# 400 slots for each expert in place of 432, in a fused kernel of attention and two feed-forward layers

## The chip, the core and the metric

The program runs on one core of a Trainium2 chip. The metric is the device time of one execution in microseconds (us). Engines are named as in the profile: PE is TensorE's matmuls and PEld its weight loads, DVE is VectorE, ACT is ScalarE, POOL is GpSimd, SP is SyncE, and a q behind a name is that engine's queue of instructions that wait, branch or issue a DMA.

## The reference

Three layers follow one another. Only what is computed matters here:

```python
# 1: attention within hash buckets; q, k, v are (2, 8, 768, 64)
mask = q_bucket[:, :, :, None] == k_bucket[:, :, None, :]
scores = np.where(mask, scale * np.matmul(q, k.transpose(0, 1, 3, 2)), -1e9)
attn = softmax(scores); x = np.matmul(attn, v)          # then (1536, 512)
# 2: a feed-forward layer, 512 -> 2048 -> 512
h = x @ w_in; g = h * sigmoid(1.702 * h); x = g @ w_out
# 3: 8 experts, each token goes to two of them
noisy_logits = x @ w_gate + np.log1p(np.exp(x @ w_noise)) * noise
top2 = np.argpartition(-noisy_logits, 2, axis=1)[:, :2]  # weights: softmax of the two
for e in range(8):
    h = np.maximum(x[mask] @ w1[e], 0.0)                 # 512 -> 1024
    out[mask] += top2_w[mask, k, None] * (h @ w2[e])     # 1024 -> 512
```

There are 1536 tokens and two experts for each, so 3072 rows of expert work, 384 for an expert on average. With the reference's own draw of the inputs (seed 0) the eight experts get 375, 391, 391, 396, 364, 373, 395 and 387 of them.

## The kernel before

**Precision.** Operands are split into two fp16 parts, hi and lo, and a product is three matmuls (hi by hi, hi by lo, lo by hi), accumulated in PSUM.

**Attention and the first feed-forward layer** run interleaved over six chunks of 256 tokens (2 batches by 3). A loop over g hands out the work in steps: scores (L252, tile s), row maximum (L261), exponential (L271), hi and lo of it (L310, L319, tile er), a transposing DMA from SP's queue (L323, et from er), and the product with v (L364, tile pv). Of the feed-forward layer L456 makes h, L474 and L486 the activation, L467 makes px. Beside this, SP loads and VectorE converts w_in and w_out, and SP writes zeros into the DRAM buffer slots (L550, L552, four blocks of 128 rows in a step) and into the output (L556). Up to step 100 (GM; the attention has 96 steps) the order on each engine is set by a scheduler that works through a timeline of its own; behind that the order is the order of the code.

**Routing** (from L572) makes the logits of a chunk, takes the two best experts and works out a slot: expert e owns rows e*CAP to e*CAP+CAP-1 of slots; tokens past CAP go to rows behind E*CAP. POOL scatters the token rows (1032 numbers of 2 bytes) into slots with an indirect DMA (L679).

**The experts.** For each expert SP loads the token rows transposed (L749, xg from slots) and their token numbers and weights (L754, L759, tile mt). The first layer L792 makes ph, 128 features by all slots of the expert, 12 matmuls for one of 8 slices; ScalarE and VectorE take it out as ht hi and lo (L802, L803). The second layer makes py for 128 slots at a time (L814, 24 matmuls of 512 columns); the slots past the last whole 128 are done as two halves of 256 columns with 64 slots each (L818, 48 matmuls). ScalarE scales py (L828) and POOL adds the rows to the output with an indirect DMA (L830). Expert 0 is done in two parts, slots 0 to 255 ahead of the last chunk's routing and the rest behind it; experts 1 to 7 are done in one. The weights w1 and w2 of the next expert are loaded (L721, L724) and split (L735, L736) under the current one. All of this stands in an order written by hand.

```python
def parts(e):
    return ((0, REG), (REG, CAP)) if e < EA else ((0, CAP),)      # REG = 256, EA = 1
...
nc.tensor.matmul(ph[:, :c1 - c0], w[:, ws, d * FE + f * 128:d * FE + f * 128 + 128],
                 xg[e, p][:, xs * HP + d, :], ...)                # L792; c0, c1 = parts(e)[p]
...
for i in range(-(-E * CAP // 512)):
    at(PARAM["I0"] + PARAM["IS"] * i, init_slots, i)              # 512 rows of slots in a step
...
most = nc.values_load(cnt_i[0:1, E:E + 1], min_val=0, max_val=N)
with tc.If(most > CAP):                                           # the overflow rows
```

**The overflow.** At the end a branch runs only if some expert has more than CAP tokens. It loads such an expert's weights again through one buffer, gathers up to 128 overflow rows at a time, and does both layers for them (from L1034 on).

Of the kernel before, what the change touches and what calls it, by code (L numbers as in the profile page):

```python
# [20 lines left out]
FF = 2048  # L21
E = 8
FE = 1024
CAP = 432
REG = 256
OV = N - CAP
NF = CAP // 128
NR = CAP - 128 * NF
NO = N + 128 + 64 - NR
# [30 lines left out]
def fused(ctx: ExitStack, tc: tile.TileContext, q, k, v, proj, w_in, w_out, w_gate, w_noise, noise,  # L60
# [451 lines left out]
    iota_e = consts.tile([128, 3, E], F32)  # L512
    for i, (b0, st_) in enumerate(((0, 1), (0, CAP), (7 * CAP, OV - CAP))):
        nc.gpsimd.iota(iota_e[:, i], pattern=[[st_, E]], base=b0, channel_multiplier=0,
# [31 lines left out]
    def init_slots(i):  # L546
        sl = slots[i * 512:min(i * 512 + 512, E * CAP)].rearrange("(k p) c -> p k c", p=128)
        n = sl.shape[1]
        for k_ in range(n):
            nc.sync.dma_start(sl[:, k_, :2 * DM].rearrange("p (u c) -> p u c", c=256),  # L550
                              zeros[:, None, :].to_broadcast([128, 2 * DM // 256, 256]))
        nc.sync.dma_start(sl[:, :, 2 * DM:], blank[:, None, :].to_broadcast([128, n, ROW - 2 * DM]))  # L552
# [13 lines left out]
    def route(ci):  # L566
# [56 lines left out]
        for c in range(2):  # L623
# [36 lines left out]
        yield  # L660
        nc.vector.scalar_tensor_tensor(ov, pq, float(CAP), iota_e[:, 2:3].to_broadcast([128, CT, E]),
                                       op0=OP.is_ge, op1=OP.mult)
# [478 lines left out]
```

## Time and profile before

| what | us |
|---|---|
| median of 3 runs | 852.13 (850.34 to 854.86) |
| the profiled execution | 851.51 |
| its span, first to last instruction | 849.4 |
| TensorE busy | 734.0 (86%) |
| VectorE busy | 541.0 (64%) |
| ScalarE busy | 443.5 (52%) |
| GpSimd busy | 270.9 (32%) |
| mean granted TensorE clock | 0.956 of 2.4 GHz |

The profile is of one execution. Its page gives busy shares over the whole span, which mixes three stages; so the span is also cut into stretches, and for the last stage the chain of waits tells which work followed which without a break. Times in the trace count from the first instruction.

The granted clock has two levels, 1.0 (2.4 GHz) and 0.5 (1.2 GHz); a stretch's figure is the mean. A matmul's own record overlaps those of its neighbours, so the time that a row of matmuls takes is read from the chain, and a record's duration is not its spacing.

### The profile page before, as it was taken

How to read it: one execution, taken by the hardware profiler on the slowest of the kernel's cores; microseconds unless marked ns; L12 is line 12 of the kernel's file. 1: busy time of each engine (PE TensorE's matmuls, PEld its weight loads, DVE VectorE, ACT ScalarE, POOL GpSimd, SP SyncE). 2: the span in 40 equal slices, each digit the busy share in tenths (PEclk: the TensorE clock that was granted, in tenths of full speed). 3: DMA queues.
4: the chain of work that ended last, by engine and by line, in shares of the span. 5: the costliest groups of instructions: out<-in, count | busy, mean ns of one | idle time of the engine just before them, and what ended most of it. 6: DMA issues, size and time to landing. Idle time of an engine off the chain costs nothing. (4 is left out here: it accounts for less than half of the span.)

```text
span 849.4 us, 14814 instructions
## 1 busy us (share of the span) xinstructions
PE 734.0 (86%) x5398; PEld 447.3 (53%) x5399; DVE 541.0 (64%) x1327; ACT 443.5 (52%) x859; POOL 270.9 (32%) x272
## 2 busy tenths in 40 slices
PE   1577658878988989798999999879999999999994
PEld 1354336435754665475567585556455554545542
DVE  8998679987896888568778527444543625335110
ACT  3777657657766686467467335244443434425210
POOL 6355437743334154214312143041021121211212
PEclk9988979998999999989999999989999999999997
DMA  8999998998999999976777634587865757766212
GB/s 205 227 253 230 210 223 179 220 212 173 179 155 214 161 190 194 223 134 106 149 131 122 139 108 122 177 200 167 221 145 168 209 120 194 156 172 162 38 15 36
DMA packets 285453, 141.03 MB, mean 166 GB/s; under 512 B 231552, under 2 KB 264384, under 8 KB 285376
## 3 DMA queue, kind: packets, MB, share of 16 engines
q1 hardware_dynamic: 278848, 126.37, 68.4%
q0 software_dynamic: 6528, 13.68, 9.2%
q8 instruction: 43, 0.70, 0.4%
q14 instruction: 34, 0.28, 0.1%
HBM read 61.49 MB, written 24.25 MB: 101 GB/s over the span
## 5 line engine op out<-in xcount | busy, mean ns | idle before, releaser
L792 PE MATMUL ph<-xg,ew 128*128 128x432 f16 (+2 forms) x864 | 146.8, 334 | 8.7 <-DMA xg<-slots 8.7
L456 PE MATMUL h<-xt,wi 128*128 128x256 f16 x1152 | 139.8, 276 | 2.0 <-DVE th L486 1.7
L467 PE MATMUL px<-wo,gt 128*128 128x512 f16 x576 | 134.9, 388 | 7.2 <-ACT wo L441 3.9
L736 DVE SCALAR_TENSOR_TENSOR ew<-w,ew 128x1024 f16<-128x1024 f32 x64 | 78.0, 1228 | 89.9 <-ACT ew L735 89.9
L830 POOL DMA_INDIRECT out_dram<-yo,ti x32 | 51.9, 1621 | 232.4 <-ACT yo L828 163.1
L814 PE MATMUL py<-ew,ht 128*128 128x512 f16 x576 | 125.8, 379 | 0.0
L456 PEld LDWEIGHTS <-wi 128*128 128x128 f16 x1152 | 112.1, 99 | 24.8 <-issue 5.5
L792 PEld LDWEIGHTS <-ew 128*128 128x128 f16 x864 | 85.3, 101 | 68.3 <-issue 6.4
L252 PE MATMUL s<-kt,qt 128*128 128x512 f16 (+1 forms) x384 | 90.6, 362 | 18.6 <-ACT e L271 14.6
L271 ACT ACTIVATE e<-s,mx 128x768 f32<-128x768 f32 x96 | 85.7, 894 | 34.0 <-DVE mx L262 19.7
L501 POOL TENSOR_TENSOR gt<-th,gt 128x512 f16<-128x512 f32 x48 | 60.2, 1254 | 114.9 <-ACT gt L500 111.3
L467 PEld LDWEIGHTS <-gt 128*128 128x128 f16 x576 | 55.9, 99 | 73.7 <-issue 10.6
L261 DVE TENSOR_REDUCE mx<-s 128x1 f32<-128x768 f32 x96 | 90.7, 949 | 6.3 <-PE s L252 6.1
L814 PEld LDWEIGHTS <-ht 128*128 128x128 f16 x576 | 56.3, 98 | 67.2
L319 DVE SCALAR_TENSOR_TENSOR er<-e,mx,er 128x768 f16<-128x768 f32 x68 | 71.2, 1049 | 24.3 <-ACT er L310 22.6
L310 ACT ACTIVATE er<-e,mx 128x768 f16<-128x768 f32 x68 | 63.3, 934 | 38.1 <-DMA et<-er 24.2
L802 ACT ACTIVATE ht<-ph 128x432 f16<-128x432 f32 (+2 forms) x72 | 35.3, 490 | 82.2 <-PE ph L792 82.2
L803 DVE SCALAR_TENSOR_TENSOR ht<-ph,ht 128x432 f16<-128x432 f32 (+2 forms) x72 | 40.0, 556 | 55.3 <-ACT ht L802 54.6
L828 ACT ACTIVATE yo<-py,wv 128x512 f32<-128x512 f32 (+1 forms) x32 | 20.3, 633 | 103.3 <-PE py L814 54.7
L735 ACT ACTIVATE ew<-w 128x1024 f16<-128x1024 f32 x64 | 66.3, 1047 | 2.5 <-DMA w<-in_moe_w_dram 2.5
L364 PE MATMUL pv<-et,vt 128*64 128x256 f16 x720 | 53.8, 283 | 13.9 <-DMA et<-er 13.9
L252 PEld LDWEIGHTS <-qt 128*128 128x128 f16 x384 | 37.1, 104 | 49.0 <-issue 26.5
(192 smaller groups left out, 930.0 us busy)
## 6 DMA issues: line engine op xcount, KB each, us to landing
w<-in_moe_w_dram SPq DMA_DIRECT2D x64, 512.0 KB
wraw<-in_moe_w_in_dram SPq DMA_DIRECT2D x16, 512.0 KB
wraw<-in_moe_w_out_dram SPq DMA_DIRECT2D x16, 512.0 KB
slots<-zeros SPq DMA_DIRECT2D x27, 256.0 KB
v<-in_v_dram SPq DMA_DIRECT2D x24, 192.0 KB
out_dram<-zeros SPq DMA_DIRECT2D x13, 256.0 KB
k<-in_k_dram SPq DMA_DIRECT2D x16, 192.0 KB
q<-in_q_dram SPq DMA_DIRECT2D x48, 64.0 KB
```

Source lines behind the costliest of these rows:

```text
L252: nc.tensor.matmul(ps[:, n0 * 128:n1 * 128], qt[:, s, h, t, :], kt[:, s, h, n0:n1, :].rearrange("p c t -> p (c t)"), start=(s == 0), stop= ...
L261: nc.vector.reduce_max(mx[:, 0:1], st[g]["ps"][:, :S], axis=AX.X)
L271: nc.scalar.activation(e32, st[g]["ps"][:, :S], AF.Exp, scale=0.125, bias=st[g]["mx"][:, 1:2], accum_out=sms[b, cc, hp][:, 2 * h + t:2 * h ...
L310: nc.scalar.activation(er[:, 0], st[g]["e"], AF.Copy, scale=r)
L319: nc.vector.scalar_tensor_tensor(er[:, 1], d["e"], d["mx"][:, 3:4], er[:, 0], op0=OP.mult, op1=OP.subtract)
L456: nc.tensor.matmul(ph[:, a, :], wi[ws][:, d, f0:f0 + 128], xt[:, d, xs, :], start=(d == 0 and ws == 0 and xs == 0), stop=(d == HP - 1 and ...
L467: nc.tensor.matmul(px, gts[ci, f // 2][:, gs, f % 2, t * 128:t * 128 + 128], wo[ws][:, f, :], start=(f == 0 and gs == 0 and ws == 0), stop ...
L501: nc.gpsimd.tensor_tensor(gt[:, 1], th, gt[:, 0], op=OP.subtract)
L735: nc.scalar.activation(hi, x, AF.Copy, scale=SW1 if j == 0 else SW2)
L736: nc.vector.scalar_tensor_tensor(lo, x, SW1 if j == 0 else SW2, hi, op0=OP.mult, op1=OP.subtract)
L792: nc.tensor.matmul(ph[:, :c1 - c0], w[:, ws, d * FE + f * 128:d * FE + f * 128 + 128], xg[e, p][:, xs * HP + d, :], start=(d == 0 and ws = ...
L814: nc.tensor.matmul(py, ht[:, f, hs, t * 128:t * 128 + 128], w[:, ws, f * DM:(f + 1) * DM], start=(i == 0), stop=(i == n - 1))
```

## The change

CAP goes from 432 to 400. What is worked out from it changes with it: OV, the rows for one expert's overflow, from 1104 to 1136; NF, the whole tiles of 128 slots, stays 3; NR, the slots past them, goes from 48 to 16; NO, the rows of the output with its padding, from 1680 to 1712. No instruction of the experts is added or taken away; they have other shapes.

```diff
 E = 8
 FE = 1024
-CAP = 432
+CAP = 400
 REG = 256
 OV = N - CAP
 NF = CAP // 128
```

In the order of the instructions three places matter.

SP's queue, in the attention part, at the last step of init_slots (before; slots are the expert rows in DRAM, qt, er and et belong to attention, xrt to the routing):

```order
L550 DMA slots<-zeros 128x4x256 x3
L552 DMA slots<-blank 128x3x8
L167 DMA_TRANSPOSE qt<-qsa 128x4x128
L323 DMA_TRANSPOSE et<-er 128x12x128 x2
L167 DMA_TRANSPOSE qt<-qsa 128x4x128
L120 DMA q_2247<-in_q_dram 128x128 x2
L323 DMA_TRANSPOSE et<-er 128x12x128 x2
L124 DMA k_2442<-in_k_dram 128x384
```

The same place now:

```order
L550 DMA slots<-zeros 128x4x256
L552 DMA slots<-blank 128x8
L167 DMA_TRANSPOSE qt<-qsa 128x4x128
L323 DMA_TRANSPOSE et<-er 128x12x128 x2
L167 DMA_TRANSPOSE qt<-qsa 128x4x128
L120 DMA q_2245<-in_q_dram 128x128
L323 DMA_TRANSPOSE et<-er 128x12x128
L120 DMA q_2245<-in_q_dram 128x128
```

Two of the zeroing writes are gone (3200 rows are 6 steps of four blocks and one block), and from here on the loads of q and k and the transposes of et stand in another order.

TensorE, shortly behind that place (before; pb is for the hash buckets, wo and gt make px):

```order
L178 LDWEIGHTS qt
L178 MATMUL pb<-pq,qt 128x6
L364 LDWEIGHTS vt
L364 MATMUL pv<-et,vt 64x256
L252 LDWEIGHTS qt
L252 MATMUL s<-kt,qt 128x512
L252 LDWEIGHTS qt
L252 MATMUL s<-kt,qt 128x256
```

The same place now:

```order
L178 LDWEIGHTS qt
L178 MATMUL pb<-pq,qt 128x6
L467 LDWEIGHTS gt
L467 MATMUL px<-wo_99,gt 128x512
L467 LDWEIGHTS gt
L467 MATMUL px<-wo_98,gt 128x512
L364 LDWEIGHTS vt
L364 MATMUL pv<-et,vt 64x256
```

Matmuls of px have moved ahead of the product with v and of the scores. Blocks of rows are exchanged in this way on every engine until the end of the attention part, and none on TensorE between there and the end of the experts.

SP's queue in the expert part, expert 0's second part and expert 1 (before; w are the raw weights):

```order
L724 DMA w_7146<-in_moe_w_dram 128x2x512
L749 DMA_TRANSPOSE xg<-slots 128x8x176
L754 DMA mt<-slots 128x8
L759 DMA mt<-slots 48x8 x2
L724 DMA w_7224<-in_moe_w_dram 128x2x512
L749 DMA_TRANSPOSE xg<-slots 128x8x432
```

The same place now:

```order
L724 DMA w_7144<-in_moe_w_dram 128x2x512
L749 DMA_TRANSPOSE xg<-slots 128x8x144
L754 DMA mt<-slots 128x8
L759 DMA mt<-slots 16x8 x2
L724 DMA w_7222<-in_moe_w_dram 128x2x512
L749 DMA_TRANSPOSE xg<-slots 128x8x400
```

Here nothing has moved (the weight loads differ by the numbers of their buffers alone); the loads from slots have 32 rows less each.

## Rows read from the trace of the kernel before

**Rows 1.** The page: the span, and busy us, share of it, instructions.

```profile
span 849.4 us, 14814 instructions
...
PE 734.0 (86%) x5398; PEld 447.3 (53%) x5399; DVE 541.0 (64%) x1327; ACT 443.5 (52%) x859; POOL 270.9 (32%) x272
```

**Rows 2.** Busy us by stretch; behind them granted TensorE clock, DMA share, GB/s.

```profile
187.00:250.00 63.00, 54.16 (x476) 37.32 (x475) 54.76 (x167) 46.07 (x97) 24.09 (x23) 0.92 0.95 169
250.00:300.00 50.00, 45.53 (x414) 28.76 (x413) 37.42 (x106) 31.97 (x67) 13.96 (x14) 0.97 1.01 188
300.00:350.00 50.00, 44.54 (x361) 27.52 (x360) 39.57 (x124) 31.71 (x69) 22.70 (x22) 1.00 0.99 201
350.00:400.00 50.00, 42.61 (x369) 30.75 (x368) 36.09 (x90) 31.71 (x67) 15.03 (x15) 0.92 0.78 143
400.00:467.00 67.00, 65.85 (x535) 42.99 (x533) 53.79 (x148) 41.35 (x80) 15.26 (x14) 0.98 0.71 129
...
538.50:567.00 28.50, 23.45 (x162) 15.38 (x163) 14.31 (x57) 9.96 (x21) 8.54 (x9) 0.93 0.62 181
567.00:587.50 20.50, 20.42 (x182) 16.19 (x182) 7.39 (x28) 6.52 (x13) 2.51 (x2) 0.85 0.83 181
...
731.10:767.00 35.90, 35.90 (x219) 18.90 (x218) 15.52 (x26) 14.33 (x20) 6.13 (x5) 1.00 0.72 168
```

**Rows 3.** Chain of waits from 555 us: start, us, what (xN: pieces in a row).

```profile
562.00 5.04 DMA xg<-slots
...
567.08 12.47 PE ph L792 x108
...
695.22 17.63 PE ph L792 x96
712.84 15.54 PE py L814 x72
728.38 2.74 PE py L818 x48
...
818.37 10.37 PE py L814 x48
...
830.18 4.86 DMA out_dram<-yo,ti
```

**Rows 4.** Chain of waits, 500 to 560 us.

```profile
503.41 10.50 PE h L456 x96
...
534.34 4.13 DMA xg<-slots
...
557.84 4.14 DMA slots<-xr,si
```

**Rows 5.** The page's DMA issues: out<-in, queue, count, KB each.

```profile
slots<-zeros SPq DMA_DIRECT2D x27, 256.0 KB
```

**Rows 6.** Timeline of 180 to 193 us: start, us, engine, line, instruction.

```profile
182.07 1.99 SPq L550 DMA_DIRECT2D slots<-zeros  x3
```

**Rows 7.** Busy us by stretch, just ahead of the moved rows (columns as in rows 2).

```profile
150.00:185.00 35.00, 28.82 (x196) 15.43 (x194) 32.66 (x57) 23.16 (x44) 20.46 (x17) 0.95 1.04 226
```

**Rows 8.** TensorE's waits, 187 to 467 us: us in total, times, longest.

```profile
PE pv L364 <- DMA et<-er: 9.0, 7, 4.3
PE s L252 <- ACT e L271: 4.4, 9, 1.0
```

**Rows 9.** Groups by shape: count | busy us, mean ns | idle before, releaser.

```profile
L792 PE MATMUL ph<-xg,ew 128*128 128x432 f16 x672 | 124.0, 346 | 0.0
...
L736 DVE SCALAR_TENSOR_TENSOR ew<-w,ew 128x1024 f16<-128x1024 f32 x64 | 78.0, 1228 | 89.9 <-ACT ew L735 89.9
...
L735 ACT ACTIVATE ew<-w 128x1024 f16<-128x1024 f32 x64 | 66.3, 1047 | 2.5 <-DMA w<-in_moe_w_dram 2.5
...
L792 PE MATMUL ph<-xg,ew 128*128 128x256 f16 x96 | 12.6, 297 | 3.8 <-DMA xg<-slots 3.8
...
L792 PE MATMUL ph<-xg,ew 128*128 128x176 f16 x96 | 10.3, 287 | 4.9 <-DMA xg<-slots 4.9
```

## The prediction

> **What bounds the kernel now.** I read the busy shares first, then the busy time by stretch, then the chain of waits in the stretch that the change touches most, then the groups by shape, and last what TensorE waits for in the attention part.
>
> The page's busy line puts TensorE at 734 of 849.4 us, but that is an average over stages with different limits, so it decides nothing [rows 1]. The stretches do [rows 2]. From 587.5 us to 828.8 us TensorE is busy without a gap, 35.90 of 35.90 us for each expert, at the full granted clock (1.00, 2.4 GHz), while VectorE has 15.5 and ScalarE 14.3 us of work in the same 35.9 and the DMA share is 0.72. Nothing but TensorE's own columns sets the end there. The chain of waits says the same and names the lines [rows 3]: an expert is 96 L792 matmuls in 17.63 us, 72 L814 matmuls in 15.54 us and 48 L818 halves in 2.74 us, one behind the other, with no wait of another engine between them. In front of it, 538.5 to 567 us is a chain of latencies (routing, a scatter into slots, the transposing load xg), and the stretch from 187 to 467 us is a mixed one: TensorE idles 8.8, 4.5, 5.5, 7.4 and 1.2 us in the five rows [rows 2].
>
> **The profiled execution and the median.** That execution took 851.51 us, of which 849.4 are span and 2.1 lie around it; the median shown is 852.13, 0.6 more. I make the sum against 851.51 and add 0.6 at the end.
>
> **The change part by part.** One constant falls from 432 to 400. What follows from it:
>
> *1. L792 on the seven experts that run in one part.* 672 matmuls have 400 columns in place of 432. What a column costs is read from the chain, where the work is end to end: 96 matmuls of 256 columns take 10.50 us, 109.4 ns each [rows 4]; 96 of 432 take 17.63 us, 183.6 ns; 72 of 512 take 15.54 us, 215.8 ns [rows 3]. The slope is 0.422 ns a column from 256 to 432 and 0.402 from 432 to 512. 400 lies in the first interval, so 32 columns are 13.5 ns and 672 of them 9.1 us; by the other slope 8.7 us. I take **9.0 us**. All of it is on the path, since no other engine is near: VectorE and ScalarE work less than half of the period there [rows 2].
>
> The Trainium skill, page "TensorE: Matmul & The Clock Gate", section "Back-to-back issue gap", gives two rules for this: a sustained stream of weight loads and matmuls at about 81 ns a matmul at 128 columns and 131 ns at 512, and for the isolated gap columns over 2.4 GHz plus 2.5 ns. By the first an estimate for 32 columns is 4.2 ns and the 768 changed matmuls would save only 3.2 us; by the second 13.3 ns and 10.2 us. The first speaks against this change; the trace's 215.8 ns at 512 columns agrees with the second and not with the first.
>
> *2. L792 on expert 0's second part.* 96 matmuls go from 176 to 144 columns. The chain shows 108 matmuls in 12.47 us from 567.08 us on, the last 12 of them already expert 1's [rows 3]; without these (12 x 0.1836 = 2.2) the 96 take 10.27 us, 107 ns each, in a stretch whose granted clock is 0.85, so partly at 1.2 GHz. At the full level 32 columns are 13.5 ns, 1.3 us for 96; at the lower one twice that, 2.6. TensorE waited 4.9 us for xg just before, so the low stretch is at the beginning, and time saved there only brings more of the matmuls into it; what falls away at the end runs at the full level. I take **1.3 us**.
>
> *3. Transposing loads and slot zeroing.* Expert 0's second xg is on the chain, 5.04 us for 176 rows, where the first took 4.13 us for 256 [rows 3, 4]. The rows alone would give 5.04 x 32/176 = 0.9 us less; that more rows took less time says that rows are not what it waits for, so the bounds are 0 and 0.9 and I take **0.3 us**. The other seven are issued an expert ahead, under 35.9 us of TensorE's work; if that cover were gone they would cost as much as this one, 5 us each. Of the zeroing, two of 27 writes of 256 KB fall away near 182 us [rows 5, 6]: 0.5 MB at that stretch's 226 GB/s is 2.3 us of the DMA engines' time, at a share of 1.04 [rows 7]. It is a gain only if TensorE's next wait is for a DMA behind them: bounds 0 and 2.3 us, taken as 0, because TensorE waits for transposes of et only 9.0 us in 7 places of the 280 us that follow [rows 8].
>
> *4. Work that shrinks under cover.* L802 and L803, which take L792's result out of PSUM, handle 400 columns; both hide under TensorE's 12 matmuls for the next slice (12 x 0.170 = 2.0 us), and were that cover gone, TensorE would have waits in the chain, where there are none [rows 3]. L814 and L818 keep their counts and shapes: the last tile still covers 64 slots, of which 16 instead of 48 are new. The last scatters, 20.6 us behind the last whole L814 tile, keep their number and size, so the tail behind 828.7 us is moved and not changed.
>
> *5. The order of the attention part.* The missing zeroing makes the scheduler put everything from about 182 us to 480 us into another order, on all engines; the order after that is written by hand and stays. No instruction is added. The rows of the order shown with the change have one unit's pv and scores behind matmuls of px instead of ahead of them; further on the scores stand 20 to 78 rows earlier and h later. That can go either way, and no row of before shows the new order. I bound it by the idle shares of the four rows from 187 to 400 us, 14.0, 8.9, 10.9 and 14.8% [rows 2]. TensorE idles 26.2 of these 213 us; at the best of the shares it would be 19.0 (a gain of 7.2), at the worst 31.5 (a loss of 5.3). I take **0**, since the four rows already are four orders of nearly the same work, and their mean is what stands there now.
>
> **The sum.** 9.0 + 1.3 + 0.3 = 10.6 us. 851.51 - 10.6 = 840.9; with the 0.6 to the median 841.5 us.
>
> **The rivals.**
>
> *The new order costs TensorE more than the old one.* For it: between 187 and 467 us TensorE waits in short pieces for transposes of et and for ScalarE and VectorE [rows 8], and VectorE has 54.8 of 63 us of work in the first row [rows 2], so a row moved forward delays another. Against it: from 400 us on TensorE has a stock of px and h and idles 1.2 us in 67. If 187 to 400 us idled at the 17.7% of the stretch just ahead (28.8 busy of 35 [rows 7]), that is 37.6 us, 11.4 more: **853 us**. Half of that gives 847. Its mirror image, an order that closes the gaps by more than 7.2 us, gives **under 834**.
>
> *Another unit takes over in the expert stage.* The period falls from 35.9 to 34.6 us. Were the 4 MB of weights for each expert already at their limit, the stage would keep its period and only parts 2 and 3 remain: **850.5 us**. Against it: the DMA share is 0.72 in the period shown and VectorE is at 43% [rows 2].
>
> *Columns are cheaper than the chain says.* The mean durations by shape differ by less: 346 ns at 432 columns, 297 at 256, 287 at 176 [rows 9]. By these slopes 32 columns are 8.9 ns, and 4.0 ns between 176 and 256: 6.0 + 0.4 + 0.3 = 6.7 us, **845 us**. The Trainium skill's first rule above (same page and section) points this way. Against it: these records overlap (96 of 346 ns would be 33 us, and the chain fits them into 17.63), so they measure depth and not spacing.
>
> *Slower than before: the overflow path runs.* At the end one branch asks whether any expert has more than 400 tokens. It runs 128 rows of such an expert again, loading all its weights through one buffer. Per expert: 8 times 512 KB at 168 GB/s (3.1 us), L735 (1.05) and L736 (1.23) in turn [rows 2, 9], 43 us; a gather and a transpose at 4.1 and 5.0, 96 matmuls at 107 ns, 24 at 216 ns and a scatter at 4.9 [rows 3, 4], 29 us. Some 70 us on top of 841.5: **912 us**. It decides with the 401st token of one expert. Worked out from the reference's own draw, the experts get 375, 391, 391, 396, 364, 373, 395 and 387 tokens, so four are missing; what speaks for it is only that the kernel's arithmetic may place a token differently, or that another draw is timed. The same number would tell that the change doesn't do what it says.
>
> **How the numbers follow.** Forecast 0.63 (834 to 846.5 us); the new order costs more than 5 us 0.17; it gains more than 7 us 0.08; another unit takes over 0.05; cheaper columns 0.03; overflow 0.04. The likeliest is 841.5. The range from 834 to 850 leaves out most of the gain beyond 7 us (0.07), the dearer half of the order's loss (0.08) and the overflow (0.04). Half a per cent, which is about what a measurement of this kernel can tell from no change, is 4.3 us: faster means under 847.9, slower over 856.4. Faster: 0.63 + 0.08 + 0.03 and a third of the order's loss, 0.78 rounded down; slower: the overflow and the far end of the order's loss, 0.06; the rest, 0.16, is within.
>
> **What the profile after would show.** Part 1: L792 in the chain at 16.3 us for 96, and 34.6 us from one expert to the next at clock 1.00; if it is 17 us or more, the slope is wrong. Part 2: the 108 matmuls in about 11 us. Part 3: xg ahead of them within 4 to 5.1 us. Part 4: L814 and L818 unchanged at 15.54 and 2.74, and some 20.6 us behind the last whole tile. Part 5: the time at which the first L792 matmul starts, 538.5 now; every microsecond by which it starts elsewhere is the order's doing, and the forecast is wrong by just that. Matmuls of the branch at the end would mean the overflow.

## The result

The changed kernel takes 842.83 us (median of 8 runs, 840.05 to 848.53) against 853.07 us of the kernel before (8 runs beside it, 850.34 to 854.86): ratio 0.9888, 95% interval 0.9857 to 0.9918. The forecast was 841.5 us, faster. The profiled execution took 843.4 us, of which 841.3 are span. A ratio is an estimate of its own from the runs of both kernels and can differ by 0.001 from the quotient of the two medians. One execution of the old order with 400 slots, of 958.89 us at a mean granted clock of 0.749 where its other four had 0.947 to 0.952, is left out of that experiment's median.

The chain of waits from 560 us on, the changed kernel (start, us, what), answers to [rows 3]:

```profile
559.92 4.25 DMA slots<-xr,si
564.19 4.91 DMA xg<-slots
...
569.15 10.97 PE ph L792 x108
...
588.15 5.29 PE ph L792 x32
593.44 9.01 DMA xg<-slots
...
602.59 2.19 PE ph L792 x12
604.77 15.54 PE py L814 x72
...
657.68 16.35 PE ph L792 x96
674.03 15.54 PE py L814 x72
689.57 2.74 PE py L818 x48
692.31 16.35 PE ph L792 x96
...
810.50 10.37 PE py L814 x48
```

96 matmuls of L792 take 16.35 us where they took 17.63, L814 and L818 are unchanged to the hundredth, and an expert takes 692.31 - 657.68 = 34.63 us in place of 35.91. Between expert 1's matmuls stands something new: the load of xg for expert 2's tokens is on the chain from 593 to 602 us. The 9.01 us are the load's, most of them under matmuls that don't need it; expert 1's period, 588.15 to 623.06, is 34.91 us, so TensorE lost some 0.3 us to it.

The stretches ahead of the experts, the changed kernel (busy us of PE, PEld, DVE, ACT, POOL; granted clock, DMA share, GB/s), answer to [rows 2]:

```profile
187.00:250.00 63.00, 50.13 (x487) 35.74 (x486) 54.07 (x155) 43.48 (x93) 21.91 (x21) 1.00 0.88 159
250.00:300.00 50.00, 41.70 (x358) 25.10 (x357) 38.77 (x109) 31.31 (x66) 17.74 (x18) 0.97 0.95 173
300.00:350.00 50.00, 45.55 (x371) 29.54 (x368) 41.32 (x128) 34.00 (x73) 21.92 (x21) 0.97 0.96 201
350.00:400.00 50.00, 44.11 (x410) 32.71 (x409) 35.71 (x94) 32.95 (x67) 15.43 (x15) 0.97 0.86 163
400.00:467.00 67.00, 61.45 (x517) 40.92 (x516) 50.22 (x144) 41.45 (x79) 16.94 (x14) 1.00 0.76 129
```

TensorE idles more here than before (37.1 us in 187 to 467 us, 27.3 before), at a higher granted clock (1.00 where it was 0.92 in the first row). The two work against each other, and the first matmul of the experts starts at 540.7 us, 2.2 us later than before.

The profiled pair adds up so, after minus before: +2.2 us to the first L792; -0.1 from there to expert 0's second part, the new xg included (28.45 us against 28.57); -1.5 for its 108 matmuls (10.97 against 12.47); -8.4 from 588.15 to the end of the last whole L814 tile at 820.9 (232.72 us against 241.16); -0.2 in the tail. Up to rounding that is the 8.1 us of span.

### The profile page after: what moved, and what is told of

Read it like the earlier page. It is cut to its first block, busy times and chain, and to the rows that moved or that the text cites. A ratio compares the mean times of both kernels' runs of the same rounds, so it can differ in the third digit from the quotient of the medians.

```text
span 841.3 us, 14817 instructions
## 1 busy us (share of the span) xinstructions
PE 723.4 (86%) x5398; PEld 446.7 (53%) x5399; DVE 538.3 (64%) x1327; ACT 443.0 (53%) x859; POOL 277.7 (33%) x272
## 5 line engine op out<-in xcount | busy, mean ns | idle before, releaser
L792 PE MATMUL ph<-xg,ew 128*128 128x400 f16 (+2 forms) x864 | 136.5, 322 | 9.2 <-DMA xg<-slots 9.2
L830 POOL DMA_INDIRECT out_dram<-yo,ti x32 | 56.1, 1753 | 218.0 <-ACT yo L828 135.7
L814 PE MATMUL py<-ew,ht 128*128 128x512 f16 x576 | 125.8, 379 | 0.0
L792 PEld LDWEIGHTS <-ew 128*128 128x128 f16 x864 | 83.7, 101 | 60.3 <-issue 6.9
L501 POOL TENSOR_TENSOR gt<-th,gt 128x512 f16<-128x512 f32 x48 | 62.9, 1311 | 121.3 <-ACT gt L500 121.0
L814 PEld LDWEIGHTS <-ht 128*128 128x128 f16 x576 | 56.4, 98 | 67.0
L802 ACT ACTIVATE ht<-ph 128x400 f16<-128x400 f32 (+2 forms) x72 | 33.5, 466 | 75.5 <-PE ph L792 75.5
L803 DVE SCALAR_TENSOR_TENSOR ht<-ph,ht 128x400 f16<-128x400 f32 (+2 forms) x72 | 37.7, 525 | 51.2 <-ACT ht L802 51.0
L364 PE MATMUL pv<-et,vt 128*64 128x256 f16 x720 | 51.0, 281 | 12.4 <-DMA et<-er 11.4
```

Source lines behind the costliest of these rows:

```text
L501: nc.gpsimd.tensor_tensor(gt[:, 1], th, gt[:, 0], op=OP.subtract)
L814: nc.tensor.matmul(py, ht[:, f, hs, t * 128:t * 128 + 128], w[:, ws, f * DM:(f + 1) * DM], start=(i == 0), stop=(i == n - 1))
```

## The experiments

Each ratio is to runs of the kernel before on the same chip: a median of 851.76 us (22 runs) beside the first four experiments, 854.23 (13 runs) beside CAP 384 and the zeroing begun one step later, 854.06 (11 runs) beside the last series.

**The old order with 400 slots.** Slots are zeroed as far as with 432, and with that every engine has the order of before ahead of the branch.

```diff
-        sl = slots[i * 512:min(i * 512 + 512, E * CAP)]
+        sl = slots[i * 512:min(i * 512 + 512, E * 432)]
-    for i in range(-(-E * CAP // 512)):
+    for i in range(-(-E * 432 // 512)):
```

> CAP is 400 everywhere, but 3456 rows of slots are zeroed as with 432, so that the order of the attention part on every engine is that of the kernel before; only the widths of the expert part are new. Theory 'columns': the narrow matmuls make the whole gain, 10.3 to 10.9 us, and the order nothing: ratio 0.9875, first L792 matmul within 0.5 us of the 538.5 of before, 34.62 us an expert. Theory 'order costs': the new order of the changed kernel loses some 2 us (its first L792 matmul stood at 540.7), so this kernel is 2 us faster than the changed one: ratio 0.985 to 0.9865. Theory 'order gains': this kernel is slower than the changed one, ratio over 0.991.

Measured: 841.8 us (median of four runs), ratio 0.9883 (0.9856 to 0.9909). That is the changed kernel's own gain, and an expert takes 657.00 - 622.37 = 34.63 us in the chain:

```profile
622.37 16.35 PE ph L792 x96
638.72 15.54 PE py L814 x72
654.26 2.74 PE py L818 x48
657.00 16.34 PE ph L792 x96
```

So the narrow work alone gives the gain. The first L792 matmul stood at 539.5 us, 1.0 us later than before and not within the 0.5 expected. The interval doesn't exclude that the new order costs 2 us; the next experiment decides it.

**The new order with the old widths.**

```diff
-        n = c1 - c0
+        n, pad = c1 - c0, 32 if (e, p) != (0, 0) else 0
-        x = m2.tile([128, 2 * HP, n], ...)
+        x = m2.tile([128, 2 * HP, n + pad], ...)
-        nc.sync.dma_start_transpose(x, slots[r0:r0 + n, :2 * DM])
+        nc.sync.dma_start_transpose(x, slots[r0 - pad:r0 + n, :2 * DM])
-                nc.tensor.matmul(ph[:, :c1 - c0], ...
+                nc.tensor.matmul(ph0[:, :c1 - c0 + pad], ...          # ph = ph0[:, pad:]
```

> The changed kernel with its new order in the attention part, but each L749 load and each L792 matmul (expert 0's first part apart) is 32 columns wider again, 432 and 176; the additional columns belong to the neighbour's slots and are not used. So it is the new order alone, with the old matmuls. Theory 'columns': no difference from before, ratio 1.000 (0.997 to 1.003), 35.9 us an expert. Theory 'order costs': ratio 1.002 to 1.004, first L792 matmul 1 to 3 us later than 538.5. Theory 'order gains': ratio under 0.997.

Measured: 850.94 us, ratio 1.0000 (0.9983 to 1.0017). With the old widths nothing is left of the gain, although the order, the two missing zeroing writes and the narrower L802 and L803 are all there. The interval is 1.4 us to either side, so a cost of the order of 2 us lies outside it. The first L792 stood at 537.4 us in the profiled run, 1.1 us ahead of before, where the profiled pair had suggested 2.2 us behind.

The chain of the experts, new order with old widths:

```profile
656.58 17.63 PE ph L792 x96
674.20 15.54 PE py L814 x72
```

**Half the step.** CAP 416, in the old order.

> CAP 416 with the old order of the attention part: half the step. Theory 'columns': half the gain, 5.2 us, ratio 0.994, 35.27 us an expert (16 columns less at 13.5 ns for 32: 672 x 6.75 ns = 4.5 us, and 0.6 us in expert 0's second part). The rival 'columns are cheaper than the chain says' would give 3.3 us, and one by which another unit takes over below some width would show most of the 400 slots' gain here already, ratio under 0.991.

Measured: 846.03 us, ratio 0.9941 (0.9926 to 0.9957). In its chain 96 matmuls take 16.99 us and an expert 35.27 us, the forecast's figure:

```profile
618.96 16.98 PE ph L792 x96
635.95 15.54 PE py L814 x72
654.23 16.99 PE ph L792 x96
```

So the saving is proportional to the columns: 17.63, 16.99 and 16.35 us at 432, 416 and 400.

**The tokens of an expert loaded earlier**, in the old order (the zeroing as in the first experiment).

```diff
-T0=12, T1=17, EL=10
+T0=12, T1=17, EL=12
```

> The old order with CAP 400, and the L749 load of an expert is issued two places earlier (EL 12 in place of 10), ahead of two weight loads. In the changed kernel the load for expert 2 ended TensorE's one wait in the expert part (9.01 us of it in the chain, at 593 to 602 us). If that load was late because it stood behind two weight loads, the chain holds no xg after 590 us here, expert 1's period is 34.6 instead of 34.9 us, and the whole is 0.3 us faster than the old order alone, less than can be timed. If the wait was another, the chain still holds it.

Measured: 840.54 us, ratio 0.9870 (0.9846 to 0.9893). The wait for expert 2's tokens is gone from the chain, and expert 1's period is 34.54 us (587.82 to 622.36) instead of 34.78 us with the old order alone:

```profile
563.85 13.62 DMA xg<-slots x2
577.60 2.19 PE ph L792 x12
...
587.82 16.26 PE ph L792 x96
604.08 15.54 PE py L814 x72
...
622.36 16.35 PE ph L792 x96
```

The gain of 0.2 us is near the forecast 0.3 and too small to time. Expert 1's period is 34.54 us in all three profiled runs with the earlier load, and 34.78, 34.82 and 34.91 in three of the four with 400 slots without it; in the fourth (zeroing begun one step later) it is 34.54 too, so the wait doesn't stand in every run. The chain shows a second such wait that this edit doesn't reach: expert 1's tokens, behind expert 0's, end a short wait of TensorE (0.6 us) at 577.6 us.

**The overflow path.** CAP 384, where five experts have more tokens than slots.

> CAP 384: five of the eight experts (391, 391, 396, 395 and 387 tokens) now have more rows than slots, so the branch at the end runs for five. It prices the rival 'the overflow path runs', forecast at 72 us for each expert. Without the branch the expert part shrinks further: 16 columns less and no L818 halves, 34.6 - 0.65 - 2.74 = 31.2 us an expert, some 27 us over all, and one scatter of 5.5 us less at the end, about 810 us. With it: 810 + 5 x 72 = 1170 us. If the branch is cheaper than thought (its weight loads overlap), 1000 to 1100; if another unit limits the experts below 34 us, the periods stay above 32 us.

Measured: 1316.84 us, ratio 1.5441 (1.5382 to 1.5499). The first half of the expectation held: with 16 columns less and no L818, from 618 us on TensorE goes from one expert to the next without a gap in 649.12 - 617.98 = 31.14 us (31.2 forecast), so no other unit takes over even there (timeline, PE: start, us, line):

```profile
617.98 15.76 PE L792 MATMUL ph<-xg,ew 128*128 128x384 f16 x96
633.58 15.70 PE L814 MATMUL py<-ew,ht 128*128 128x512 f16 x72
649.12 15.76 PE L792 MATMUL ph<-xg,ew 128*128 128x384 f16 x96
```

The second half did not: the branch costs 911.25 - 813.57 = 97.7 us for an expert, not 72. Its timeline, from one expert's first instruction to the next one's:

```profile
813.57 0.23 DVE L1050 TENSOR_SCALAR sel<-iota_e,cur 128x8 f32<-128x8 f32 x1 [22.60 <-PEq L1049]
...
860.74 1.22 DVE L1066 SCALAR_TENSOR_TENSOR wo<-x,wo 128x1024 f16<-128x1024 f32 x1 [4.74 <-ACT wo L1065]
...
883.11 1.58 POOL L1109 DMA_INDIRECT out_dram<-yo,ints  x1 [18.95 <-ACT yo L1108]
909.10 0.15 DVE L1113 TENSOR_SCALAR cur<-cur 128x1 f32<-128x1 f32 x1 [29.37 <-issue]
911.25 0.23 DVE L1050 TENSOR_SCALAR sel<-iota_e,cur 128x8 f32<-128x8 f32 x1 [2.00 <-PEq L1049]
```

The eight weight loads take 47.4 us up to 862.0 (43 forecast) and the rows themselves 22.7 us up to the end of the scatter's issue at 884.7 (29 forecast). Then 24.4 us pass in which nothing is computed. The loop over blocks of 128 overflow rows has nine turns and only the first has rows. The trace shows the other eight: VectorE's branch of L1069, the test whether a block has rows, comes eight times in these 24.4 us (instructions of the line: count, ns min/median/max, first and last start):

```profile
L1069 DVEq COMPARE_BRANCH  x8: 124/124/124, 889.7 to 907.1; - x8
```

That is 17.4 us for seven steps, 2.5 us for an empty turn and 19.9 for eight. The other 4.5 us lie between the scatter's issue and the first empty turn.

**Other orders**, zeroing begun one step later (I0 17 in place of 16), with 432 and with 400 slots. These are two orders and not one: with 400 slots two writes fewer are placed, and from 187 us on the engines' instructions stand in another order than with 432.

```diff
-R1=2, I0=16
+R1=2, I0=17
```

> The kernel before with its zeroing of slots begun one step later (I0 17 in place of 16): same work, same widths, another order of the attention part on every engine. Theory 'order is even': ratio 0.996 to 1.004, as in the run with the new order and the old widths. Theory 'the old order was a good draw': slower by 3 us or more, ratio over 1.004. The forecast had bounded what an order does to the time by -7 to +5 us.

> The changed kernel, zeroing begun one step later: a third order with 400 slots. Theory 'columns and an even order': ratio 0.985 to 0.991 like the changed kernel and the one with the old order. If orders matter by several microseconds, this one or the 432 one falls outside.

Measured: with 432 slots 850.83 us, ratio 0.9961 (0.9938 to 0.9984), just inside the even case; with 400 slots 841.23 us, 0.9870 (0.9834 to 0.9906). So an order can be worth some 3 us here (1.4 to 5.3 by the interval), and the old one was no good draw. With 400 slots three orders were timed (the old one, the changed kernel's and, as a third, this one), and they are not told apart.

**The changed kernel and the earlier loads on one chip.**

> The changed kernel once more, on one chip beside the two that load xg earlier, since the first comparisons came from different chips and overlap. Theory 'columns': 9 to 11 us under before again, ratio 0.987 to 0.990.

> The old order with 400 slots and the earlier L749 loads, again. If the wait for expert 2's tokens is all that it takes away, 0.3 us under the old order and 0 to 1 us beside the changed kernel, inside the measurement (ratio 0.987 to 0.989). If the lower median of the first comparison (0.9870 against 0.9888) was more than scatter, it stays 1.5 us under the changed kernel.

> The third order (zeroing one step later) with the earlier L749 loads, the candidate for the fastest. Theory 'order is even': 0.987 to 0.989, not told apart from the other two. If the third order is a better draw, as its 0.987 may say, 1.5 to 3 us under the changed kernel.

Measured: the changed kernel again 841.41 us, 0.9850 (0.9819 to 0.9881), a little under the range expected, whose lower part the interval holds; old order with the earlier loads 844.24 us, 0.9870 (0.9848 to 0.9892); third order with the earlier loads 840.53 us, 0.9844 (0.9820 to 0.9868). The second did not stay under the changed kernel, so its better first median was scatter. The third is the fastest median of all, but its interval overlaps with the changed kernel's: faster than the kernel before is shown, faster than the changed one is not.

## Why the prediction was right, point by point

The forecast gain was 10.6 us; by the ratio it is 9.6 us, with an interval from 7.0 to 12.2. Such a time alone can't tell which parts were right; the chains and the experiments can.

**Part 1, the columns: right.** Forecast 9.0 us for 672 matmuls. The full periods gave 17.63 - 16.35 = 1.28 us for 96, 13.3 ns a matmul, between the two slopes' 12.9 and 13.5; 672 of them are 9.0. Of this the profiled pair kept 8.4 us behind 588 us and 0.2 in the 12 that belong to the stretch ahead; 0.3 went to the wait for expert 2's tokens (34.91 us for expert 1, 34.62 for the next). The Trainium skill's first rule ("TensorE: Matmul & The Clock Gate", section "Back-to-back issue gap"), by which 768 matmuls would, as an estimate, have saved 3.2 us, is refuted here: 170.3 ns at 400 columns (16.35 us for 96), 183.6 at 432. The second rule, columns over 2.4 GHz plus 2.5 ns, gives as an estimate 169.2 and 182.5 and agrees.

**Part 2: right in the profiled pair.** 10.97 against 12.47 us, of which 0.2 belongs to expert 1's 12 matmuls: 1.3, as forecast. Its premise, that the stretch at the lower clock lies at the beginning, holds in the traces: before, the granted clock is 0.50 from 567 to 573 us and 1.00 from there; after, it is 0.50 from 569 to 573 us and back at 1.00 from 575. What the step did not look at is what comes next: expert 0's second part can end before expert 1's tokens have landed. With the old order and 400 slots TensorE waited for xg three times, 10.7 us, where before it waited twice, 8.7 us.

TensorE's waits from 530 us on (us in total, times, longest), the kernel before:

```profile
PE ph L792 <- DMA xg<-slots: 8.7, 2, 4.9
```

The old order with 400 slots:

```profile
PE ph L792 <- DMA xg<-slots: 10.7, 3, 4.6
```

The third wait, 1.5 us, is for expert 1's tokens. That the shorter matmuls bring it about is not shown. It stands in four of the seven profiled runs with 400 slots (1.5, 0.6, 0.6 and 6.0 us) and in neither of the changed kernel's own two; with the matmuls of 432 slots it stands in one of three, the run with zeroing begun one step later (0.9 us of wait; chain):

```profile
564.59 14.55 DMA xg<-slots x2
579.27 2.35 PE ph L792 x12
```

**Part 3: the mechanism right, the term a little large.** The second xg took 4.91 in place of 5.04 us, 0.1 and not 0.3: rows are indeed not what it waits for. Even the 0.1 is within scatter: from its issue to the first matmul behind it the seven profiled runs with 144 rows take 4.4 to 5.3 us, and the three with 176 rows 4.8 to 5.1. The sentence that the other loads are issued an expert ahead, under 35.9 us of TensorE's work, was wrong: in the trace of before expert 2's load is issued at 593.1 us and its first matmul starts at 602.8, a cover of 9.7 us, and the others have 11 to 12. In the changed kernel these are 9.2 us for expert 2 and 10 to 11 for the others, and a load takes about as long (9.01 us on its chain). That little of this became a wait in the profiled pair is luck, since the forecast hadn't looked at it.

**Part 4: right.** L814 and L818 kept 15.54 and 2.74 us, and the tail behind the last whole tile 20.4 us (20.6 before).

**Part 5, the order: right in size, with more scatter than was said.** It was taken as 0, with bounds from -7 to +5. The new order with the old widths puts it at 0 within 1.4 us, the order with 432 slots and zeroing one step later at -3.3. The profiled pair alone would have misled: its +2.2 us to the first L792 lies within what one and the same order does from run to run. Profiled runs with the old order reached that matmul at 538.5, 539.5, 540.4, 541.5 and 536.5 us, those with the changed kernel's order at 540.7, 540.6 and 537.4.

**The rivals.** Another unit taking over was refuted down to a period of 31.1 us; cheaper columns by the half step; the overflow did not run with 400 slots (the trace has no matmul of the branch), and had it run for one expert, it would have cost about 98 us and not 70. The largest missing term there is the eight empty turns of the loop, 19.9 us, which no row of before could show.

## What to carry to other kernels

Where the chain shows one engine's work end to end, price a change of shape by the spacing in the chain (us of a row by its count) and not by the mean duration of a record. When a constant also moves the order that a scheduler makes, run the two halves apart, old order with new shapes and new order with old shapes: two profiles alone cannot separate a microsecond or two of order from the scatter between runs. And read the cover of a load from its issue to its first use and not from the period: here it was some 10 to 12 us of a period of 35.9. Work that is shortened under a load shortens its cover too.

## What the runs showed of the hardware

In one run a late load cost more than its wait. The second series' profiled run of the old order with earlier loads took 851.91 us, where that kernel's median is 844.24. Its stretch from 570 to 600 us, beside the same stretch of the same kernel in the first series (columns as above), second series first:

```profile
570.00:600.00 30.00, 23.96 (x199) 16.84 (x198) 10.17 (x36) 8.87 (x17) 2.27 (x2) 0.80 0.76 135
```

```profile
570.00:600.00 30.00, 28.84 (x245) 19.29 (x244) 15.47 (x38) 13.02 (x23) 3.94 (x2) 0.97 0.85 188
```

and its chain there:

```profile
565.12 4.40 DMA xg<-slots
569.56 14.85 DMA xg<-slots
584.55 4.16 PE ph L792 x12
```

Expert 1's tokens landed 14.9 us behind expert 0's; TensorE had waited 6.0 us in one piece, where it waited 0.6 us in the first series. The granted clock of the stretch was 0.80 (0.50 from 583 to 587 us), and the 12 matmuls that followed took 4.16 us in place of 2.19, 347 ns each, the 1.2 GHz level. So this one load cost its wait and then about 2 us more at the lower clock. Why it took so long in this run is open. The changed kernel's own runs spread over 8.5 us and those of before beside it over 4.5; whether such waits make the difference is open, and no run was made to show it.
